# A DMA hold on GpSimd: gradient loads tied to the landing of an x transpose, and a fourth y/z buffer

## Chip, cores, metric

One core of one Trainium2 chip. The metric is the device time of one launch in microseconds, the median of repeated runs. The kernel before takes 2145.0 us (2144.54 to 2149.26 in three runs). All times compared below are of fast runs (not over 1.5% above the fastest of the same kernel) unless it is said otherwise.

## The reference

Window attention over a 256 x 256 image with 384 channels, windows of 8 x 8 tokens, one head; forward output and the gradients of x, wqkv and wo, all bf16.

```python
qkv = xw @ wqkv                       # xw: x cut into windows of 64 tokens
p = softmax(einsum('bqc,bkc->bqk', q, k) * C ** -0.5)
o = einsum('bqk,bkc->bqc', p, v) @ wo
_out, _vjp = jax.vjp(_f, x, wqkv, wo)
return (_out, *_vjp(grad_out))
```

## The kernel before

The image is worked through in 128 quads of eight windows (four 128-token tiles of 96 KB). Each quad needs x and grad_out both with tokens on the partitions (`xq`, `dq`) and with channels on the partitions (`xT`, `dT`). DMA transposes issued by SP turn them; `tok` turns the projections y/z back and `UT` turns a product needed for dx. Four quads are in the pipeline at once, at different steps.

```python
def load(st):
    bp, t0 = st["at"]
    st["xq"] = xq = grp.tile([P, QUAD, C], BF16, tag="xq", name="xq", bufs=2 * GQ + 4)
    st["dq"] = dq = qp.tile([P, QUAD, C], BF16, tag="dq", name="dq", bufs=6)
    for t in range(QUAD):
        nc.sync.dma_start(out=xq[:, t, :], in_=dram_tile(x, bp, t0 + t))
        nc.gpsimd.dma_start(out=dq[:, t, :], in_=dram_tile(grad_out, bp, t0 + t))
# ... cut ...
for i in range(-1, n + 2):
    d, c, b, a = get(i - 2), get(i - 1), get(i), get(i + 1)
    if i + 2 > 0 and get(i + 2) is not None:
        to_channels(get(i + 2), "dq", "dT")       # SP: DMA transpose
        to_channels(get(i + 2), "xq", "xT")       # SP: DMA transpose
    if get(i + LEAD) is not None:                 # LEAD = 3
        load(get(i + LEAD))                       # SP: x, GpSimd: grad_out
    if c is not None:
        to_tokens(c)                              # SP: DMA transpose tok
    step(d, c, b, a)                              # PE, ACT, DVE; GpSimd stores; SP: UT
```

GpSimd's queue also issues all stores of out_0 (from `osb`, four buffers) and out_1 (from `dsb`). The program gives GpSimd these instructions in one order, so a load that waits there holds up the stores behind it.

Of the kernel before, what the change touches and what calls it, by code (L numbers as in the profile page):

```python
# [11 lines left out]
BF16 = mybir.dt.bfloat16  # L12
F32 = mybir.dt.float32

P = 128
WIN = 8
WT = WIN * WIN
QUAD = 4
# [4 lines left out]
def kernel(  # L23
# [12 lines left out]
    nc = tc.nc  # L36
    _, H, W, C = x.shape
    CK = C // P
# [5 lines left out]
    LEAD = 3  # L44
# [3 lines left out]
    qp = ctx.enter_context(tc.tile_pool(name="qp", bufs=2))  # L48
# [52 lines left out]
    def dram_tile(ap, bp, t):  # L101
        return ap[0, 2 * WIN * bp:2 * WIN * (bp + 1), WIN * t:WIN * (t + 1), :]

    LO, HI = slice(0, WT), slice(WT, P)

    def load(st):
        bp, t0 = st["at"]
        st["xq"] = xq = grp.tile([P, QUAD, C], BF16, tag="xq", name="xq", bufs=2 * GQ + 4)
        st["dq"] = dq = qp.tile([P, QUAD, C], BF16, tag="dq", name="dq", bufs=6)
        for t in range(QUAD):  # L110
            nc.sync.dma_start(out=xq[:, t, :], in_=dram_tile(x, bp, t0 + t))
            nc.gpsimd.dma_start(out=dq[:, t, :], in_=dram_tile(grad_out, bp, t0 + t))  # L112

    def to_channels(st, src, name):
        st[name] = dst = qp.tile([P, QUAD, CK, P], BF16, tag=name, name=name, bufs=3 if name == "xT" else 2)
        nc.sync.dma_start_transpose(out=dst[:].rearrange("p t m k -> p (t m) k"),
                                    in_=st[src][:].rearrange("p t c -> p (t c)"))
# [3 lines left out]
    def product(out, lhsT, rhs, start, stop):  # L121
        if split[0]:
            for h in (LO, HI):
                nc.tensor.matmul(out[h], lhsT=lhsT[:, h], rhs=rhs, start=start, stop=stop)  # L124
        else:
            nc.tensor.matmul(out, lhsT=lhsT, rhs=rhs, start=start, stop=stop)  # L126

    def project(st, kind, mo):
        if kind == 0 and mo == 0:
            st["yz"] = qp.tile([P, CK, QUAD, 4, WT], BF16, tag="yz", name="yz", bufs=3)  # L130
        yz = st["yz"]
        wgt, src = ((BT_sb, st["dT"]), (A_sb, st["xT"]))[kind]
        pj = ring.tile([P, QUAD, 2, WT], F32, tag="r", name="pj")
        for m in range(CK):
            product(pj[:].rearrange("p t w k -> p (t w k)"), wgt[:, m, mo * P:(mo + 1) * P], src[:, :, m, :],
                    m == 0, m == CK - 1)
        if kind == 0:
            nc.scalar.copy(out=yz[:, mo, :, 0:4:3, :], in_=pj[:])  # L138
        else:
            nc.scalar.copy(out=yz[:, mo, :, 1:3, :], in_=pj[:])  # L140

    def to_tokens(st):
        st["tok"] = tok = qp.tile([P, CK, QUAD, 2, P], BF16, tag="tok", name="tok")
        nc.sync.dma_start_transpose(out=tok[:].rearrange("p m t b k -> p (m t b) k"),
                                    in_=st["yz"][:].rearrange("p m t s k -> p (m t s k)"))
# [132 lines left out]
    def gf_group(sts):  # L278
        n = len(sts) * QUAD
        for f, rn in enumerate(("Uq", "Wq")):  # L280
            for ma in range(CK):
                pw = ring.tile([P, C], F32, tag="r", name="pg")
                for i in range(n):
                    st, t = sts[i // QUAD], i % QUAD
                    product(pw[:], st["xq"][:, t, ma * P:(ma + 1) * P], st[rn][:, t, :], i == 0, i == n - 1)
                nc.vector.tensor_tensor(out=GF_acc[:, f, ma, :], in0=pw[:], in1=GF_acc[:, f, ma, :], op=ALU.add)  # L286
                yield

    def filler(n):
        while n and fill:  # L290
            try:
                next(fill[0])
                n -= 1
            except StopIteration:
                fill.pop(0)

    def step(d, c, b, a):
        def on(st):
            return (lambda f, *r: f(st, *r)) if st is not None else (lambda f, *r: None)
        D_, C_, B, A = on(d), on(c), on(b), on(a)  # L300
        B(scores)
        B(soft, 0)
        B(soft, 1)
        B(values, 0)
        B(values, 1)
        B(values, 2)
        B(soft, 2)
        B(values, 3)
        B(soft, 3, 0)
        A(project, 0, 0)  # L310
        A(project, 0, 1)
        B(soft, 3, 1)
        A(project, 0, 2)
        B(soft, 4)
        A(project, 1, 0)
        B(soft, 5)
        A(project, 1, 1)
        A(project, 1, 2)
        filler(1)
        pw = C_(attend, (2, 3))  # L320
        pt = B(turn)
        if b is not None:
            turn_end(b, pt)
        C_(to_channels, "Uq", "UT")
        C_(attend_end, (2, 3), pw)
        split[0] = True
        D_(dx, (0, 1))
        filler(1)
        split[0] = False
        pw = B(attend, (0, 1))  # L330
        B(attend_end, (0, 1), pw)
        D_(dx, (2, 3))
# [4 lines left out]
    get = lambda i: sts[i] if 0 <= i < n else None  # L337
    with tc.manual_schedule(engines=MANUAL):
        for i in range(min(LEAD - 1, n)):
            load(sts[i])  # L340
        to_channels(sts[0], "dq", "dT")
        to_channels(sts[0], "xq", "xT")
        held = []
# [3 lines that stand above are left out]
                to_channels(get(i + 2), "dq", "dT")  # L347
                to_channels(get(i + 2), "xq", "xT")
            if get(i + LEAD) is not None:
                load(get(i + LEAD))  # L350
            if c is not None:
                to_tokens(c)
            step(d, c, b, a)
            if c is not None:
                held.append(c)
            if held and (len(held) == GQ or i == n):
                fill.append(gf_group(held))
                held = []
            if 0 <= i - 2:
                sts[i - 2] = None  # L360
        filler(1 << 30)
# [62 lines left out]
```

## Time and profile before

| | before |
|---|---|
| time, median | 2145.0 us |
| PE busy | 2021.4 us, 95% |
| DMA queue shares, SP + GpSimd | 85.6% + 27.5% |
| SP's cycle: one quad, dT to dT | 16.41 us |
| of it in issues / waiting before dT / other gaps | 15.58 / 0.23 / 0.60 us |
| PE's shortest spacing of quads (the first three, shorter, left out); mean of all | 14.83; 16.26 us |

SP's cycle is read out of the trace instruction by instruction (quads 11 to 120), not from a ready view. SP's cycle is the sum of how long its eight issues of a quad last and of the gaps between them. I read a long issue as one whose descriptors the DMA engines don't take at once (tok's lasts 4.08 to 6.78 us for the same work); a gap is a wait for something not yet there. The prediction shows the lines of the profile.

### The profile page before, as it was taken

To read this page: it belongs to the slowest core of one execution; us is meant where nothing else is said; L and a number is where in the kernel's file an instruction comes from. 1 tells how busy PE (TensorE), PEld (TensorE's weight loads), DVE (VectorE), ACT (ScalarE), POOL (GpSimd) and SP (SyncE) were. 2 spreads that over 40 slices of the span, in tenths; PEclk is the share of its full clock that TensorE was granted. 3 is DMA by queue.
4 is the path that set the end of the run, shared out by engine and by line. 5 is a ranking of instruction groups with operands and counts; after the bars stand their busy time and mean duration, and the time that the engine had idled before them with its cause. 6 is when DMAs were issued, how large, how long until landed. Compare 5 with 4: busy or idle time off the path is not lost. (4 is left out here: it accounts for less than half of the span.)

```text
span 2135.8 us, 51378 instructions
## 1 busy us (share of the span) xinstructions
PE 2021.4 (95%) x19046; PEld 1183.3 (55%) x19046; DVE 1280.2 (60%) x2851; ACT 1455.3 (68%) x3213; POOL 1122.7 (53%) x2054
## 2 busy tenths in 40 slices
PE   8899999999999999999999999999999999999998
PEld 4555555555555555555555555555555555555555
DVE  6565565656565656656565665665656565665664
ACT  6667676766676667767676766766666676666673
POOL 4554555555555545545454555554555455555543
PEclk9999999999999999999999999999999999999999
DMA  9999999999999999999999999999999999999995
GB/s 210 220 225 220 217 219 211 224 221 219 215 219 213 225 206 225 218 212 222 215 218 213 216 224 211 218 220 218 216 212 221 211 220 222 222 223 211 220 208 123
DMA packets 1173339, 459.11 MB, mean 215 GB/s; under 512 B 1056864, under 2 KB 1147744, under 8 KB 1173088
## 3 DMA queue, kind: packets, MB, share of 16 engines
q1 hardware_dynamic: 1074384, 304.15, 85.6%
q0 software_dynamic: 98304, 151.39, 27.5%
q8 instruction: 149, 2.44, 0.5%
q14 instruction: 102, 0.84, 0.1%
q10 hardware_dynamic: 400, 0.29, 0.0%
HBM read 101.84 MB, written 101.84 MB: 95 GB/s over the span
## 5 line engine op out<-in xcount | busy, mean ns | idle before, releaser
L231 POOL DMA_DIRECT2D out_dram<-osb x1024 | 578.3, 571 | 682.9 <-ACT osb L249 637.3
L138 ACT CAST yz<-pj 128x512 bf16<-128x512 f32 x384 | 213.4, 588 | 360.6 <-DMA tok<-yz 328.0
L286 DVE TENSOR_TENSOR GF_acc<-pg,GF_acc 128x384 f32<-128x384 f32 x258 | 143.9, 558 | 471.8 <-PE pg L124 269.0
L249 ACT CAST osb<-po 128x384 bf16<-128x384 f32 x512 | 225.1, 501 | 211.3 <-issue 174.8
L112 POOL DMA_DIRECT2D dq<-in_grad_out_dram x512 | 270.6, 537 | 174.2 <-DMA out_dram<-osb 63.8
L233 POOL DMA_DIRECT2D out_dram<-dsb x512 | 275.4, 541 | 136.4 <-DMA out_dram<-dsb 62.4
L250 DVE CAST Uq<-pu 128x384 bf16<-128x384 f32 x512 | 264.7, 550 | 54.9 <-PE pu L242 53.0
L126 PE MATMUL pv<-B_sb,xT 128*128 128x384 bf16 x1536 | 270.6, 326 | 0.0
L126 PE MATMUL pj<-xT,A_sb 128*128 128x512 bf16 x1152 | 269.5, 379 | 0.9 <-DMA xT<-xq 0.9
L126 PE MATMUL pj<-dT,BT_sb 128*128 128x512 bf16 x1152 | 269.5, 379 | 0.0
L224 ACT CAST uq<-pv 128x384 bf16<-128x384 f32 x512 | 242.7, 475 | 35.5 <-PE pv L126 33.3
L261 ACT CAST Wq<-pw 64x384 bf16<-64x384 f32 x512 | 242.5, 474 | 9.2
L273 ACT CAST dsb<-pd 128x384 bf16<-128x384 f32 x512 | 222.0, 482 | 26.0 <-ACT Wq L261 7.5
L124 PEld LDWEIGHTS <-xq 128*64 128x64 bf16 x3024 | 204.6, 111 | 45.6
L126 PEld LDWEIGHTS <-xq 128*128 128x128 bf16 x1560 | 152.6, 98 | 114.0
L140 ACT CAST yz<-pj 128x512 bf16<-128x512 f32 x384 | 201.3, 603 | 1.2 <-PE pj L126 1.1
L126 PEld LDWEIGHTS <-A_sb 128*128 128x128 bf16 x1152 | 112.6, 98 | 137.1 <-DMA xT<-xq 1.4
L242 PE MATMUL po<-uq,PS 64*64 64x384 bf16 x1024 | 145.0, 338 | 45.9 <-ACT yz L138 45.5
L126 PEld LDWEIGHTS <-xT 128*128 128x128 bf16 x1536 | 141.5, 98 | 82.8
L124 PE MATMUL pg<-Wq,xq 128*64 128x384 bf16 x2016 | 182.0, 329 | 0.0
L166 DVE TENSOR_REDUCE mx<-sd 64x4 f32<-64x256 f32 x256 | 108.1, 422 | 122.6 <-PE sd L153 118.6
L126 PE MATMUL pg<-Uq,xq 128*128 128x384 bf16 x1032 | 181.6, 326 | 0.0
(66 smaller groups left out, 2674.9 us busy)
## 6 DMA issues: line engine op xcount, KB each, us to landing
xq<-in_x_dram SPq DMA_DIRECT2D x512, 96.0 KB, 3.7
dq<-in_grad_out_dram POOLq DMA_DIRECT2D x512, 96.0 KB, 4.8
out_dram<-osb POOLq DMA_DIRECT2D x1024, 48.0 KB, 5.3
out_dram<-dsb POOLq DMA_DIRECT2D x512, 96.0 KB, 5.5
dT<-dq SPq DMA_TRANSPOSE x128, 6.5
xT<-xq SPq DMA_TRANSPOSE x128, 5.1
tok<-yz SPq DMA_TRANSPOSE x128, 10.2
UT<-Uq SPq DMA_TRANSPOSE x128, 6.4
```

Source lines behind the costliest of these rows:

```text
L112: nc.gpsimd.dma_start(out=dq[:, t, :], in_=dram_tile(grad_out, bp, t0 + t))
L124: nc.tensor.matmul(out[h], lhsT=lhsT[:, h], rhs=rhs, start=start, stop=stop)
L126: nc.tensor.matmul(out, lhsT=lhsT, rhs=rhs, start=start, stop=stop)
L138: nc.scalar.copy(out=yz[:, mo, :, 0:4:3, :], in_=pj[:])
L140: nc.scalar.copy(out=yz[:, mo, :, 1:3, :], in_=pj[:])
L224: nc.scalar.copy(out=st["uq"][:, t, :], in_=pj[:])
L231: nc.gpsimd.dma_start(out=to[WIN * w:WIN * (w + 1)], in_=src[h, :])
L233: nc.gpsimd.dma_start(out=to, in_=src[:])
L249: nc.scalar.copy(out=osb[:], in_=po[:])
L250: nc.vector.tensor_copy(out=st["Uq"][:, t, :], in_=pu[:])
L261: nc.scalar.copy(out=st["Wq"][h, pair[1], :], in_=pw[1][o, :])
L273: nc.scalar.copy(out=dsb[:], in_=pd[:])
```

## The change

The intent: keep the gradient loads away from the transposes dT and xT and let them run beside the plain x loads that follow these. A one-element copy on GpSimd reads `xT` of the quad two on and writes into the gradient tile, so it can't run before that transpose has landed, and the loads behind it can't start before the copy.

```diff
-    def load(st):
+    def load(st, behind=None):
...
+        if behind is not None:
+            nc.gpsimd.tensor_copy(out=dq[0:1, 0, 0:1], in_=behind["xT"][0:1, 0, 0, 0:1])
         for t in range(QUAD):
...
-            st["yz"] = qp.tile([P, CK, QUAD, 4, WT], BF16, tag="yz", name="yz", bufs=3)
+            st["yz"] = qp.tile([P, CK, QUAD, 4, WT], BF16, tag="yz", name="yz", bufs=4)
...
-                load(get(i + LEAD))
+                load(get(i + LEAD), get(i + 2))
```

## The prediction

> **What bounds the kernel now.** I read the page first, then the waits, then the timeline of the SP queue, because the first two do not name one bound.
>
> ```profile
> PE 2021.4 (95%) x19046; PEld 1183.3 (55%) x19046; DVE 1280.2 (60%) x2851; ACT 1455.3 (68%) x3213; POOL 1122.7 (53%) x2054
> ...
> DMA  9999999999999999999999999999999999999995
> ...
> q1 hardware_dynamic: 1074384, 304.15, 85.6%
> q0 software_dynamic: 98304, 151.39, 27.5%
> ```
>
> PE and the DMA engines both look full. PE is not the bound: with no stall, one quad takes PE 14.83 us from its scores to the next quad's (the smallest spacing of the sd matmuls, seen in 20-odd of 127 quads), while the mean spacing is 16.26 us. What is lost shows in the waits, where ACT holds PE up because a y/z buffer still belongs to a transpose:
>
> ```profile
> ACT yz L138 <- DMA tok<-yz: 328.0, 99, 7.2
> PE po L242 <- ACT yz L138: 45.5, 72, 3.9
> ```
>
> The columns are total us, times and longest us. Why are the transposes late? This is the SP queue, one quad from dT to dT being the repeating unit (start, duration):
>
> ```profile
> 1009.94 3.12 SPq L116 DMA_TRANSPOSE dT<-dq  x1
> 1013.24 1.69 SPq L116 DMA_TRANSPOSE xT<-xq  x1
> 1014.98 2.89 SPq L111 DMA_DIRECT2D xq<-in_x_dram  x4
> 1017.98 6.78 SPq L144 DMA_TRANSPOSE tok<-yz  x1
> 1024.85 2.88 SPq L116 DMA_TRANSPOSE UT<-Uq  x1
> 1027.95 1.80 SPq L116 DMA_TRANSPOSE dT<-dq  x1
> ```
>
> It is never idle: each issue begins within 0.3 us of the end of the one before, and between 80 us and 2,078 us I find no gap over 0.4 us. It waits for no semaphore; it is busy issuing. The mean issue times are 5.44 (tok), 2.46 (UT), 2.88 (dT), 2.18 (xT) and four x loads of 0.66: 15.6 us, which with some 0.7 us between them is the whole 16.3 us quad. So the SP stream sets the pace and PE follows it. Most of that time is not forced. The same issues by tile (min/median/max ns):
>
> ```profile
> L144 SPq DMA_TRANSPOSE tok<-yz x128: 4077/5442/6779, 36.1 to 2099.2; - x128
> L116 SPq DMA_TRANSPOSE UT<-Uq x128: 1422/2477/3950, 41.3 to 2103.7; - x128
> L116 SPq DMA_TRANSPOSE dT<-dq x128: 1447/2918/3953, 9.3 to 2060.4; - x128
> L116 SPq DMA_TRANSPOSE xT<-xq x128: 1413/2229/3890, 11.1 to 2063.5; - x128
> ```
>
> At the minima a quad would take 4.1 + 1.4 + 1.4 + 1.4 + 4 x 0.55 + 0.7 = 11.2 us. The other 5 us are back-pressure, as GpSimd's queue (q0: gradient loads and both outputs' stores, 12 x 96 KB a quad) uses the same DMA engines. Stretches show how badly the two mix (last columns: DMA share, GB/s):
>
> ```profile
> 1004.50:1006.50 2.00, 2.00 (x25) 1.03 (x22) 1.93 (x4) 1.65 (x4) 1.15 (x3) 1.00 1.14 56
> 1026.00:1027.00 1.00, 1.00 (x6) 0.41 (x5) 0.95 (x3) 0.00 (x0) 0.26 (x1) 1.00 1.09 365
> 1031.00:1033.00 2.00, 1.07 (x9) 0.46 (x10) 0.81 (x2) 2.00 (x5) 0.00 (x0) 1.00 1.27 286
> ```
>
> By the packet records, the third is transposes alone, the second q0 alone with the transposes standing, and the first is tok's transposes beside a few store packets: everything in flight, next to nothing moved.
>
> **What the Trainium skill says.** "DMA: Bandwidth & Descriptors", section "Issuing engines are not separate DMA queues": transfers begun from any engine end up on the same 16 DMA engines and interleave. The trace agrees: the two queues' shares sum to 113%. The same page, "Queues, rings and completion order": an engine takes turns between queues, a packet at a time. A transpose packet (256 B) takes 18 ns in the median and 174 ns at the 99th percentile; a q0 packet of 4,608 B takes 178 ns at its fastest. A transpose packet that waits out one q0 packet would look like that. "Perfetto Trace Analysis", "Identifying Performance Opportunities": a bubble that repeats can mean too few buffers. The 99 waits of ACT for tok are such a bubble, but the next part says why I expect little from the buffer.
>
> **The change part by part.** *Fourth y/z buffer.* The write of y/z then waits for a transpose issued one quad earlier, long landed; the 328 us of ACT's wait, and PE's 45.5 + 13.4 us of waits for ACT's yz casts, go. But the SP stream does not wait for PE: its inputs (yz, dq, xq) are ready many us before it gets to them. PE therefore runs ahead by a few us once, until it stands at dx for UT (landing now 8.2 us after the start of the step that needs it about 10 us in), and then again moves at SP's pace. Alone: nothing, 0 to 10 us.
>
> *The hold.* It adds 126 one-element GpSimd copies (GpSimd's memsets in this trace took 0.1 to 0.2 us; estimate 0.2 to 0.3 us each with their semaphores, on an engine that is idle at that moment). It takes no transfer away; it moves them. Times below are from L, the landing of xT (13.0 us into PE's step in the mean). Now the four gradient loads are issued from L - 8.8 us; their data flow, some 3 us later (median from issue to first large packet 2.94 us), during the UT, dT and xT transposes. Afterwards they are issued from L + 0.4 to L + 2.5. The x loads are issued from about L - 3 to L - 0.4 and their packets run from about L - 0.9 to L + 1.8. GpSimd has been idle, so the first data come about 1 us after issue: the tail of the x loads catches perhaps 60 KB, and the rest runs beside tok, which follows at once. The intent of running beside x is met only in part. GpSimd is in order, so the stores of osb, which now run beside the x loads, fall in behind: osb at L + 2.5 to 4.8, dsb to 5.9, osb to 8.2, dsb to 9.3.
>
> To price this I cut the SP queue's data stream into phases by its own packets and fitted each phase's length, over 115 quads, to the KB of each kind of q0 traffic in it. Mean KB a quad (gradients, osb, dsb), length without q0, and us per 1,000 KB:
> x loads: 12, 134, 30; 1.95 us; 4.25, 4.79, 2.08.
> tok: 1, 115, 143; 4.62; (no gradients to fit), 1.96, 3.06.
> UT: 77, 125, 153; 2.26; 4.17, 3.25, 2.71.
> dT: 132, 7, 53; 1.27; 6.77, 9.74, 4.82.
> xT: 162, 5, 6; 1.69; 4.91, 2.60, 5.62.
> Measured lengths 2.70, 5.29, 3.40, 2.49, 2.53: 16.41 us. The reason for the differences I take to be that tok and x are issued slower than the engines could move them and leave room, and dT and xT do not.
>
> After, with my placing (x 60 gradients; tok 324 gradients and 192 osb; UT 192 dsb and 150 osb; dT 42 osb and 192 dsb; xT none), and 3.34 us per 1,000 KB for gradients in tok, which is tok's slope for all traffic together:
> x 1.95 + 0.26 = 2.21; tok 4.62 + 1.08 + 0.38 = 6.08; UT 2.26 + 0.52 + 0.49 = 3.27; dT 1.27 + 0.41 + 0.93 = 2.61; xT 1.69. Sum **15.86 us**, 0.55 less than 16.41. Over some 127 quads: **70 us**, 2145 - 70 = **2075 us**.
>
> A second reading of the same trace: sorted by q0 traffic within dT and xT, the quarter of the quads with least (142 KB) took 15.68 us a cycle, the others 16.46, 16.69 and 16.81 (316, 436, 568 KB), at nearly equal totals. After the change I place 234 KB there. That agrees in sign and size: about 0.5 us.
>
> **Rivals.** *Only moved.* If gradients cost as much beside tok as beside dT and xT (5.7 us per 1,000 KB instead of 3.34), tok grows by another 0.76 us and the sum is 16.6: no gain, 2145 to 2175. For it: tok's fit is weak (R2 0.16), a fit over whole cycles gives tok traffic 5.5 +- 2 us per 1,000 KB, and the empty stretch shown above lies in tok. Against it: the quarters.
> *A new loop.* xT's landing, copy, gradient loads, dT, xT is now a ring: 0.4 to the first issue, 1.6 to the fourth, about 4.5 to its landing (the median is 4.8), 2.9 and 2.2 for the two issues, 3 to the landing: 14.6 us, near the cycle. SP would reach dT at L + 7.8 and the gradients land at about L + 6.5. A wait of SP there of up to 2 us is filled by UT's packets still queued (2.6 us from issue to first packet), so I expect short waits and little loss. If landings stretch to 7 us beside tok, it adds up to 1 us a quad: slower, up to 2200.
> *Stores late.* osb has four buffers; stores now leave some 4 to 6 us later and would land about L + 9, against the next use at about L + 12. ACT's osb may begin to wait for DMA, but PE has slack against SP, so this costs nothing unless several us more are lost.
> *Better than placed.* If dT and xT free of q0 come down to their minima and tok swallows the gradients in its own slack, the cycle falls towards 15 us, and PE at 14.83 us becomes the bound: 1970 to 2000.
>
> **Range and chances.** The main sum says 2075, the first rival 2145 or a little over, the last 2000. The fits are correlations in one trace, so I widen both ways and move the middle a little towards no change: 2080 us, 8 in 10 for 2005 to 2150. Faster by over 2% means below 2102: 0.60. Within 2%: 0.34. Slower: 0.06.
>
> **What would show it.** Right: ACT's wait for tok on yz gone, SP still without gaps, dT and xT issues down from 2.9 and 2.2 us to about 2.3 and 1.5, tok up towards 6, spacing of the sd matmuls about 15.8 us, the PE's stalls now at dx for UT or tok. Wrong: gaps on SP before dT that a gradient load ends (the loop), tok far above 6.5 us (only moved), PE at 14.83 us throughout (SP was not autonomous, or the buffer mattered), or ACT's osb waiting for stores with PE behind it. The step I trust least is the price of gradients beside tok.

## The result, and the profile after

The changed kernel takes 2239.76 us (2225.55 to 2252.35, three runs): ratio 1.0433, 95% interval 1.0331 to 1.0535, **slower**. Ratios here are the mean time of one kernel's fast runs over the mean of the other's of the same rounds, so not quite the ratio of the quoted medians. The prediction was 2080 us in a range of 2005 to 2150.

The page of the changed kernel, busy times and DMA queues:

```profile
PE 2021.8 (90%) x19046; PEld 1127.7 (50%) x19046; DVE 1264.2 (56%) x2851; ACT 1466.8 (66%) x3213; POOL 1145.3 (51%) x2180
...
q1 hardware_dynamic: 1074384, 304.15, 80.5%
q0 software_dynamic: 98304, 151.39, 28.1%
```

The work is the same to the packet, and PE is as busy in microseconds as before; there is more time in which it waits. (The granted clock reads 0.971 after and 0.986 before; with PE's busy time the same within 0.4 us, the lost time is not there.) What SP waits for, before (total us, times, longest):

```profile
SPq L116 <- DMA dq<-in_grad_out_dram: 1.3, 2, 0.9
```

and after:

```profile
SPq L118 <- DMA dq<-in_grad_out_dram: 225.4, 235, 4.6
```

This wait was not there before. It stands in front of dT, the transpose of the gradients. The view has longer lines for SP in both kernels (before: `SPq L144 <- ACT uq L224`, 349.0 us), but most of that lies within issues: the gaps before tok sum to 19 us in the whole run before. The gaps before dT sum to 30 us before and 251 after, which bears out the line above. SP's queue after, one cycle in order of time (start, duration):

```profile
1018.98 4.38 SPq L146 DMA_TRANSPOSE tok<-yz  x1
1023.45 1.99 SPq L118 DMA_TRANSPOSE UT<-Uq  x1
1027.17 1.44 SPq L118 DMA_TRANSPOSE dT<-dq  x1
1028.79 2.87 SPq L118 DMA_TRANSPOSE xT<-xq  x1
1031.71 4.77 SPq L113 DMA_DIRECT2D xq<-in_x_dram  x4
```

UT's issue ends at 1025.44 and dT's begins at 1027.17: SP stands still for 1.7 us. Every other gap in these lines is 0.2 us or less. GpSimd in the same stretch:

```profile
1019.41 0.18 POOL L111 COPY dq<-xT 1x1 bf16<-1x1 bf16 x1 [5.10 <-PE pw L244]
1019.97 2.11 POOL L114 DMA_DIRECT2D dq<-in_grad_out_dram  x4 [0.39 <-POOL dq L111]
1022.05 2.28 POOL L233 DMA_DIRECT2D out_dram<-osb  x4
1026.42 1.08 POOL L235 DMA_DIRECT2D out_dram<-dsb  x2 [2.09 <-DMA dq<-in_grad_out_dram]
```

The copy comes 5.1 us after GpSimd's last work, the loads are issued from 1019.97 on, but their data don't flow then. Counted from the packet records of the same stretch (half-microsecond slices; transpose packets started, KB of GpSimd's queue started):

```
from     transposes  x loads  GpSimd's queue
1020.5   362         8        0 KB
1022.0   568         0        0 KB
1023.0   521         0        0 KB
1024.0   237         0        63 KB
1025.0   8           0        156 KB
1026.0   0           0        117 KB
1027.0   502         0        0 KB     gradients landed, dT issued
```

Four loads, all issued by 1022.1, move nothing until tok's transposes run out, from about 1024 on; then they and the first stores behind them have the engines to themselves while the transposes stand. The two kinds of traffic take turns in blocks.

The durations of the issues after (ns, min/median/max), and the gradient loads with their median time from issue to landing (last number, us; it was 4.8 before):

```profile
L146 SPq DMA_TRANSPOSE tok<-yz x128: 3808/4290/7587, 42.6 to 2201.5; - x128
L118 SPq DMA_TRANSPOSE dT<-dq x128: 1423/1594/2957, 9.2 to 2166.0; - x128
L118 SPq DMA_TRANSPOSE xT<-xq x128: 1431/2932/4277, 10.9 to 2167.6; - x128
...
dq<-in_grad_out_dram POOLq DMA_DIRECT2D x512, 96.0 KB, 6.0
```

Against the lines in the prediction, tok is 1.15 us and dT 1.3 us shorter, and xT is 0.7 us longer. The mean over quads (a quad's four x loads included) gives the balance: issues 14.65 us instead of 15.58, waiting before dT 1.95 instead of 0.23, other gaps 0.59: a cycle of **17.19 us instead of 16.41**. The difference of 0.78 us over 127 quads is 99 us; the measured slowdown is 95.

Two more lines of the changed kernel's waits, which a rival explanation rests on:

```profile
ACT osb L251 <- DMA out_dram<-osb: 381.0, 210, 5.9
...
PE pd L269 <- DMA tok<-yz: 78.6, 57, 6.5
```

ACT now waits for an osb buffer whose store is late, and PE waits for tok at dx.

### The profile page after: what moved, and what is told of

It reads as the page before. It is cut to its first block, busy times and chain, and to the rows that moved or that the text cites.

```text
span 2238.0 us, 51758 instructions
## 1 busy us (share of the span) xinstructions
PE 2021.8 (90%) x19046; PEld 1127.7 (50%) x19046; DVE 1264.2 (56%) x2851; ACT 1466.8 (66%) x3213; POOL 1145.3 (51%) x2180
## 5 line engine op out<-in xcount | busy, mean ns | idle before, releaser
L251 ACT CAST osb<-po 128x384 bf16<-128x384 f32 x512 | 236.5, 480 | 645.9 <-DMA out_dram<-osb 381.0
L111 POOL COPY dq<-xT 1x1 bf16<-1x1 bf16 x126 | 22.4, 178 | 608.9 <-DMA xT<-xq 400.8
L269 PE MATMUL pd<-tok,ps 128*64 128x384 bf16 x1024 | 144.8, 339 | 137.9 <-DMA tok<-yz 78.6
L252 DVE CAST Uq<-pu 128x384 bf16<-128x384 f32 x512 | 259.3, 548 | 14.7 <-PE pu L244 14.5
L275 ACT CAST dsb<-pd 128x384 bf16<-128x384 f32 x512 | 227.4, 481 | 57.5 <-PE pd L126 19.6
L226 ACT CAST uq<-pv 128x384 bf16<-128x384 f32 x512 | 233.5, 483 | 18.4 <-PE pv L128 16.6
L126 PEld LDWEIGHTS <-xq 128*64 128x64 bf16 x3024 | 191.7, 120 | 91.8
L126 PE MATMUL pd<-AT_sb,UT 128*64 128x384 bf16 x1536 | 174.0, 369 | 57.3 <-DMA UT<-Uq 56.4
L140 ACT CAST yz<-pj 128x512 bf16<-128x512 f32 x384 | 220.5, 589 | 3.9 <-PE pj L128 0.2
L142 ACT CAST yz<-pj 128x512 bf16<-128x512 f32 x384 | 201.3, 603 | 0.2
L126 PE MATMUL pg<-Wq,xq 128*64 128x384 bf16 x2016 | 195.2, 347 | 0.0
```

What stands on the lines that cost most here:

```text
L126: nc.tensor.matmul(out[h], lhsT=lhsT[:, h], rhs=rhs, start=start, stop=stop)
L140: nc.scalar.copy(out=yz[:, mo, :, 0:4:3, :], in_=pj[:])
L142: nc.scalar.copy(out=yz[:, mo, :, 1:3, :], in_=pj[:])
L226: nc.scalar.copy(out=st["uq"][:, t, :], in_=pj[:])
L251: nc.scalar.copy(out=osb[:], in_=po[:])
L252: nc.vector.tensor_copy(out=st["Uq"][:, t, :], in_=pu[:])
```

## The experiments

**Theories.** *Ring*: the hold closes a ring, from xT's landing through the copy, the gradient loads and SP's wait at dT to the issue and landing of the next xT. Measured from xT's landing, means of quads 10 to 119: first load issued at 0.72, the fourth at 2.38, the last landed at 8.65, dT issued at 8.79 us. With 1.81 for dT's issue, 0.19 for the gap and 6.4 from xT's issue to its landing (the page's median) that is 17.2 us, the whole cycle. *Contention*: bunching GpSimd's transfers makes the DMA engines slower whatever waits there are. *Late stores*: the stores behind the hold come late, osb's four buffers run out, ACT and PE fall behind. *Buffer*: the fourth y/z buffer lets PE run ahead into something worse.

A summary of all runs first; cycle, issues and waits are SP's, in us a quad, each from the profiled run of that kernel:

| run | median us | ratio to before | cycle | issues | wait at dT |
|---|---|---|---|---|---|
| before | 2145.0 | 1 | 16.41 | 15.58 | 0.23 |
| the change | 2239.76 | 1.0433 | 17.19 | 14.65 | 1.95 |
| yz_only | 2149.44 | 0.9984 | 16.47 | 15.65 | 0.23 |
| hold_only | 2274.49 | 1.0590 | 17.38 | 14.70 | 2.08 |
| hold_dT | 2179.32 | 1.0124 | 16.65 | 15.62 | 0.44 |
| hold_lead4 | 2130.02 | 0.9905 | 16.38 | 15.66 | 0.24 |
| free_lead4 | 2145.74 | 0.9972 | 16.43 | 15.71 | 0.23 |
| hold_past | 2132.89 | 0.9910 | 16.36 | 15.53 | 0.24 |
| swap_hold | 2180.47 | 1.0105 | 16.73 | 15.84 | 0.23 |
| swap_free | 2160.03 | 1.0020 | 16.56 | 15.68 | 0.22 |
| tok_split | 2269.74 | 1.0565 | 17.41 | 16.33 | 0.35 |
| split_free | 2225.32 | 1.0346 | 17.16 | 16.20 | 0.23 |
| dose_hold | 2314.56 | 1.0754 | 17.82 | 13.70 | 3.53 |
| dose_lead4 | 2088.13 | 0.9729 | 16.01 | 15.28 | 0.24 |
| lead4_9 (the same again) | 2094.42 | 0.9699 | 16.03 | 15.30 | 0.24 |
| lead4_18 | 2099.81 | 0.9729 | 16.06 | 15.30 | 0.24 |
| lead4_27 | 2392.66 | 1.1084 | 18.56 | 14.54 | 0.33 |

Also run: no_dsb, x_on_act and swap_hold_lead4, told below. In the runs made together, before itself has medians of 2149.6 to 2158.1 us.

### yz_only and hold_only: the two halves

yz_only is the kernel before with `bufs=4` for yz; hold_only is the change with `bufs=3`.

> The fourth y/z buffer alone, no hold. Loop theory (the hold makes SP wait for gradients that themselves wait behind tok): the buffer is innocent; SP sets the pace and does not wait for PE, so the time stays at 2145 us, within 2135 to 2155, and ACT's 328 us of waits for tok on yz go and turn into PE waits for tok or UT at dx. If the buffer is what slows the changed kernel (PE running ahead, stores falling into other transposes): 2200 us or more.

> The hold alone, three y/z buffers. Loop theory: as slow as the whole change or a little slower, 2225 to 2270 us, with SP waiting about 2 us a quad for the gradients before dT. If the buffer is the culprit: 2145 us.

yz_only: 2149.44 us, ratio 0.9984 (0.9959 to 1.0008): as before, within the expectation. hold_only: 2274.49 us, ratio 1.059 (1.0516 to 1.0664), just above the expected range. The buffer theory falls, and the hold alone carries the slowdown. With the hold the fourth buffer even helps, by 35 us; without it, the ring of the profiled run is longer by 0.2 us (the last gradients land at 8.85 us, dT is issued at 9.01), but why was not tested.

The packet records of yz_only show more than its time. PE runs ahead, GpSimd with it, and the gradient loads are issued 12.6 us before xT's landing instead of 8.9. So the buffer alone takes two thirds of the gradients away from dT and xT (100 KB a quad there instead of 294; the table under lead4_9 has both runs), and the time stays. Taking them away from dT and xT was what the hold was for.

### hold_lead4 and free_lead4: the ring opened, everything else kept

```diff
-    LEAD = 3
+    LEAD = 4
-  xq ... bufs=2 * GQ + 4
+  xq ... bufs=2 * GQ + 5
```

hold_lead4 is the change with this edit: the gradients are issued at the same place, after xT and before tok, but belong to the quad after the next. free_lead4 has the edit and the fourth y/z buffer without the hold.

> The whole change with x and gradients loaded one quad further ahead (LEAD 4, one more xq buffer): same hold, same place of the gradient loads between xT and tok, but the dT that needs them comes one quad later, so the ring of hold, gradients, dT, xT is opened. Loop theory: no waits of SP before dT; a quad costs SP its issues, 14.6 us now, and 0.7 us between them, so about 15.4 us a quad: 2010 to 2080 us. Contention or late-store theory: 2200 us or more, as nothing about the mixing or the stores is changed.

> Control for hold_lead4: loads one quad further ahead and four y/z buffers, without the hold. If the hold's new place for the gradients is worth something by itself, this run stays at the time before, 2140 to 2155 us, and hold_lead4's 1 per cent is the hold's. If the 1 per cent came from the longer lead, this run is at 2125 to 2135 us as well.

hold_lead4: 2130.02 us, ratio 0.9905 (0.9879 to 0.9932). SP's wait in this run, and the wait that the late-store theory goes by:

```profile
SPq L118 <- DMA dq<-in_grad_out_dram: 2.4, 2, 1.3
...
ACT osb L251 <- DMA out_dram<-osb: 260.8, 174, 4.8
```

The loads are issued 0.73 us after xT's landing and land at 8.60, as in the change (0.72 and 8.65); only nobody waits for them. The whole slowdown is gone. ACT still waits 261 us for stores, so that wait alone does not slow the kernel. This decides between ring and contention, and between ring and late stores. But the expected 2010 to 2080 us did not come: SP's issues went from 14.65 back to 15.66 us. The short issues of the changed kernel were no gain of the new place. While SP stands, the DMA engines work off what is queued and take the next descriptors faster; that is my reading of 14.65 against 15.66, and of dose_hold below. free_lead4, at 0.9972 (0.9953 to 0.999), shows that the longer lead is not what matters. Against it hold_lead4 is 0.7% faster, about 15 us, where the prediction had 70; and hold_past below, whose loads don't wait, gains as much over yz_only, so even this is not shown to come from the place.

### hold_dT: the hold on the other transpose

```diff
-  in_=behind["xT"][0:1, 0, 0, 0:1]
+  in_=behind["dT"][0:1, 0, 0, 0:1]
```

> The whole change, but the hold waits for the transpose dT of two quads on, which lands some 3 us before xT. Loop theory: the gradient loads are issued while xT is under way, pass at the border of xT and the x loads instead of behind tok, land some 5 us earlier against SP's dT, and SP's waits before dT all but vanish: 2060 to 2140 us. Contention theory (any hold packs GpSimd's traffic into fewer microseconds and the DMA engines lose more): 2200 us or more, SP without waits but with longer issues. Late-store theory (osb's four buffers): 2200 or more, with ACT's osb waiting for stores as now (381 us).

2179.32 us, ratio 1.0124 (1.0067 to 1.0182). SP's wait and the gradient loads' time to landing:

```profile
SPq L118 <- DMA dq<-in_grad_out_dram: 38.1, 46, 2.5
...
dq<-in_grad_out_dram POOLq DMA_DIRECT2D x512, 96.0 KB, 3.5
```

SP's waits fall from 225 us to 38, and most of the slowdown with them; the loads land 2.5 us sooner, no longer behind tok. Here the intent is met: by the packet records 312 of a quad's 384 KB of gradients flow in the x phase. (A phase runs from the last packet of SP's DMA before to the last packet of its own; what flows while the transposes stand counts to the phase that follows.) And it gains nothing: the kernel is still 1.2% slower than before. Against yz_only, its control, the x phase grew from 3.16 to 3.49 us and tok's from 5.19 to 5.46, UT's shrank from 3.55 to 2.95, and the issues sum to 15.62 us as ever; the wait of 0.21 us a quad that is left makes 27 us. The expected time of 2060 to 2140 us was missed.

### hold_past: the copies without the wait

```diff
-                load(get(i + LEAD), get(i + 2))
+                load(get(i + LEAD), get(i + 1))
```

> The whole change, but the copy reads the xT of one quad on instead of two quads on, which landed a quad earlier: the same 126 copies and the same instruction order on GpSimd, with no time in the wait. Loop theory: 2140 to 2160 us, as with the fourth buffer alone; SP waits for gradients below 10 us in all. If the copies themselves, or the order they force, cost the time: 2200 us or more.

2132.89 us, ratio 0.991 (0.9883 to 0.9936), a little better than expected. The copies and their order cost nothing. That they gain 0.7% over yz_only is not explained.

### swap_hold, swap_free, swap_hold_lead4: xT before dT

```diff
-                to_channels(get(i + 2), "dq", "dT")
                 to_channels(get(i + 2), "xq", "xT")
+                to_channels(get(i + 2), "dq", "dT")
```

> The whole change, with SP issuing the transpose xT before dT instead of after it. Hold, buffers, lead and bytes are as in the change, but the gradients now have from the landing of xT to the dT of the next quad about 12.8 us (16.3 us a quad + 2.9 for xT's issue - 6.4 from its issue to its landing) where they had about 7.8 and need about 8.3 (0.7 copy, 1.6 issues, 6.0 landing). Loop theory: SP's waits for gradients fall from 225 us to below 20, and the time to 2120 to 2165 us. Contention or late-store theory: 2200 us or more.

> Control for swap_hold: four y/z buffers and xT before dT, no hold. The order of two equal transposes moves no work: 2135 to 2160 us. If the order itself is worth something, this run shows it and swap_hold must be read against this one.

> hold_lead4 with xT before dT: with no ring left in either, this tells whether the hold's place for the gradients (now released while dT is under way, so nearer to the x loads) is worth more than the 1 per cent of hold_lead4. If DMA work is conserved wherever the gradients run: 2120 to 2150 us. If running truly beside the x loads is the gain that was intended: 2100 us or less.

swap_hold: 2180.47 us, ratio 1.0105 (1.0078 to 1.0131); SP's wait for gradients is 1.0 us in the whole run. As the ring arithmetic said, the last gradients land at 8.0 us and dT is issued at 13.6 us after xT's landing. So the ring opens and most of the slowdown goes, with the lead and the bytes of the change; the time is 15 us above the range, since the issues are 0.16 us longer than in swap_free (2160.03 us, 1.002). swap_hold_lead4: 2175.66 us, ratio 1.0076 (1.0054 to 1.0098), slower than both of its expectations. With no ring in either, running in the x phase (299 of 384 KB in swap_hold) is again no gain.

### dose_hold and dose_lead4: the ring made longer, closed and open

```diff
-            nc.gpsimd.tensor_copy(out=dq[0:1, 0, 0:1], in_=behind["xT"][0:1, 0, 0, 0:1])
+            for _ in range(9):
+                nc.gpsimd.tensor_copy(out=dq[0:1, 0, 0:1], in_=behind["xT"][0:1, 0, 0, 0:1])
```

> The whole change with the one-element copy done nine times in a row instead of once: every gradient load is issued later by eight more copies, 1.4 us if they follow each other at their 178 ns, more if each waits for the one before. Loop theory: the ring sets the cycle (17.2 us), so nearly all of the delay shows in each of some 126 quads: 2240 + 126 x 1.4 = about 2410 us, 2340 to 2450. Contention or late-store theory: a delay of an idle GpSimd engine changes little, 2220 to 2290 us.

> The same nine copies in hold_lead4, where the gradients have a whole quad to spare. Loop theory: nothing to delay, 2120 to 2160 us. If the delay costs as much here as in dose_hold, the ring is not what it acts through.

dose_hold: 2314.56 us, ratio 1.0754 (1.0718 to 1.079), 75 us more than the change, below the expected range. The loads are issued 1.89 us later but land only 0.71 us later, since the last one takes 5.10 us to land instead of 6.27; 0.71 us over 126 quads is 89 us. SP's wait in this run:

```profile
SPq L119 <- DMA dq<-in_grad_out_dram: 419.2, 249, 6.2
```

dose_lead4: 2088.13 us, ratio 0.9729 (0.9658 to 0.98). The same delay costs 75 us where the ring is closed and gains 42 where it is open. That settles the ring, and it contradicts what I had expected of the open one, no effect. It is also faster than both kernels.

### lead4_9, lead4_18, lead4_27: how late is best

hold_lead4 with 9 (a repeat of dose_lead4), 18 and 27 copies.

> A repeat of dose_lead4, same source, beside two longer delays. If its gain is real: 2075 to 2105 us again; if it was chance: 2130 us, as hold_lead4.

> Eighteen copies in hold_lead4: the gradients are issued some 4.6 us after xT's landing instead of 2.7 (nine copies) or 0.7 (one). In dose_lead4 the tok transpose, nearly free of other traffic, took 3.8 us of data instead of 4.7 and the gradients passed behind it. If keeping tok to itself is the gain, the best is near where they arrive at tok's end, so about as dose_lead4, 2070 to 2110 us. If any delay gains (less traffic bunched with the stores): lower still, below 2070.

> Twenty-seven copies: gradients issued some 6.6 us after xT's landing, into UT and dT, with the osb stores a further 2 us late behind them on GpSimd. If tok to itself is the gain: no better than with 18, 2090 to 2150 us, as UT, dT and xT now carry what tok was spared and ACT's osb waits longer for its buffers. If any delay gains: below 2070.

lead4_9: 2094.42 us, ratio **0.9699** (0.9675 to 0.9724); the gain is real. lead4_18: 2099.81 us, 0.9729 (0.9696 to 0.9762), the same. Where the gradients flow, in KB a quad and in SP's data phases (which are cut at SP's own packets), with each phase's length in us (two counts of one run differ by up to some 20 KB in tok and UT):

```
             x     tok          UT           dT           xT
before       2.71  5.30 (1)     3.41 (68)    2.48 (132)   2.48 (162)
yz_only      3.16  5.19 (5)     3.55 (267)   2.15 (83)    2.42 (17)
free_lead4   3.07  5.32 (5)     3.53 (284)   2.13 (75)    2.39 (8)
hold_lead4   2.49  4.70 (160)   3.82 (215)   2.33 (2)     3.03 (0)
lead4_9      2.83  3.72 (59)    3.99 (299)   2.57 (18)    2.94 (1)
lead4_18     2.91  4.31 (12)    2.82 (108)   3.32 (201)   2.72 (52)
```

With nine copies they reach the engines as tok ends. tok, left nearly alone, is 0.98 us shorter, and the others give back 0.66. So a place can matter, but it is not the one beside the x loads. Two quite different places, UT and dT, give the same time, so this is a reading for nine copies and no rule.

lead4_27: 2392.66 us, ratio 1.1084, far outside the 2090 to 2150 expected. GpSimd in this run:

```profile
1015.72 6.39 POOL L112 COPY dq<-xT 1x1 bf16<-1x1 bf16 x27
1022.47 2.11 POOL L115 DMA_DIRECT2D dq<-in_grad_out_dram  x4 [0.37 <-POOL dq L112]
1024.55 2.28 POOL L234 DMA_DIRECT2D out_dram<-osb  x4
1029.63 1.08 POOL L236 DMA_DIRECT2D out_dram<-dsb  x2 [2.80 <-DMA dq<-in_grad_out_dram]
1030.70 2.25 POOL L234 DMA_DIRECT2D out_dram<-osb  x4
1032.95 1.08 POOL L236 DMA_DIRECT2D out_dram<-dsb  x2
1034.02 6.15 POOL L112 COPY dq<-xT 1x1 bf16<-1x1 bf16 x26
```

It no longer waits for xT at all: 15.2 us of its own work and 2.8 of a wait fill the cycle. Stores come later still, PE waits 266.9 us behind ACT's osb, and SP stands 3.2 us a quad before UT. Here the late-store theory holds, once GpSimd itself is full.

### tok_split and split_free: tok in three pieces

```diff
-  one DMA transpose of all of yz into tok
+  for m in range(CK): one DMA transpose of yz[:, m] into tok[:, m]
```

> The whole change, with the tok transpose cut into three, one for each third of the channels. The packet records show GpSimd's packets passing mostly near the borders between two transposes, and the held gradients land late (median 5.8 us) because tok, the longest, stands in front of them. If that is what stretches the ring: gradients land about 1 us sooner, SP's wait for them before dT falls from 225 us to below 120, and the time to 2150 to 2200 us. If their lateness has another cause (start-up of GpSimd's queue, bandwidth alone): waits and time as in the change, 2225 to 2260 us.

> Control for tok_split: fourth y/z buffer, tok cut in three, no hold. If the cut itself is what kept tok_split slow (its SP issues sum to 16.4 us a quad where uncut kernels without waits have 15.6): 2230 to 2280 us, as slow as tok_split. If the cut is free: 2145 us, and then tok_split's time is unexplained by the ring.

tok_split (the change with this edit): 2269.74 us, ratio 1.0565 (1.0524 to 1.0606). The gradients land at a median of 4.6 us instead of 6.0 (the 5.8 of the expectation has dT's own landings mixed in) and SP's wait for them falls to 23.1 us from 225.4, as expected if tok stands in their way; the packet records agree, as the first load of a quad starts to move data 1.53 us after its issue (median), in the change 3.59 us and in hold_dT, beside the x loads, 1.32 us. The time does not fall. split_free (the edit without the hold): 2225.32 us, 1.0346, 5 us below its range. Three smaller transposes make SP's issues dearer by 0.55 us a quad (16.20 against 15.65 in yz_only), which hides what the ring gave back: the hold costs 44 us with tok cut (2269.74 against 2225.32) and 90 us uncut (2239.76 against 2149.44). So the pair supports the reason for the late landing, and half of the cost goes with it; SP's waits account for some 15 us of the 44 that are left, the rest is not explained.

### no_dsb and x_on_act: what sets SP's pace

no_dsb is the kernel before without most stores of out_1. Its output is wrong, which doesn't matter for the time. x_on_act is yz_only with the x loads issued by ACT (`nc.scalar.dma_start`).

> Wrong result on purpose: the kernel before with the stores of out_1 left out from the second band of windows on, a third of GpSimd's traffic. If the DMA engines' total work sets the pace (16.3 us a quad, of which some 1.4 to 1.7 us for 384 KB), PE becomes the bound at 14.83 us a quad or nearly: 1950 to 2010 us. If PE or a chain of waits sets the pace: 2100 us or more.

> Fourth y/z buffer, no hold, and the x loads issued from ScalarE's queue instead of SP's: takes four issues of 0.7 us a quad out of the SP stream without changing a byte. If the SP queue's own issuing is the pace, a quad falls to PE's 14.83 us: 1960 to 2030 us. If the DMA engines' work is the pace, the transposes' issues stretch by what was freed and the time stays within 2 per cent of 2145 us.

no_dsb: 2092.81 us in one run of unknown state, cycle 16.05 us. With a third of GpSimd's traffic gone, the cycle is 0.36 us shorter where 1.4 to 1.7 were expected. Neither expectation holds: as far as one run goes, traffic costs, but not by the KB. x_on_act: 2229.7 us, ratio 1.0317 (1.0237 to 1.0397), also outside both expectations. SP has four issues fewer, and its transposes' issues stretch from 12.74 us a quad (yz_only) to 16.49. So SP's issuing time is not what the pace is made of; but the load on ACT, whose casts PE waits for, changed as well, so the slowdown itself is not explained by this run.

## Why the prediction was wrong

**What sets the pace: right as far as tested.** SP's stream led before and leads after: what was lost stands in its gaps before dT. Its cycle accounts for the slowdown, 0.78 us x 127 = 99 us against 95 measured; that sum alone does not show who leads, since in the long run all engines have the same cycle. (The prediction's "no gap over 0.4 us" is a slip: I count ten gaps of 0.42 to 0.56 us between 80 and 2,078 us, too few to matter.)

**Fourth buffer: right in time.** "Alone: nothing, 0 to 10 us"; measured 0.9984. Missed was that GpSimd runs ahead with PE, so that the buffer moves the gradients by itself.

**The hold, where the gradients flow: both the places and the prices were wrong.** The sum of 15.86 us failed first in its placing. I placed 324 KB of gradients beside tok and nothing in xT; in the change 192 KB flowed beside tok and 176 beside UT. hold_lead4 has the place without the ring, and its phases sum to 16.37 us. tok is shorter than summed (4.70 against 6.08), xT carries some 300 KB of stores and takes 3.03 us instead of 1.69, and UT carries 215 KB of gradients and takes 3.82 instead of 3.27. The prediction's prices at the KB that did flow give 16.38 us for hold_lead4, which is right; but they give 15.94 for yz_only, where 16.47 was measured, and 16.94 for lead4_9, where it was 16.0. A price list that misses by 0.5 to 0.9 us could not carry a gain of 0.55. In the changed kernel's own trace the same fit gives 10.4 us per 1,000 KB for gradients in tok instead of 3.34; I take it that phases that end when GpSimd's block gets its turn have their length and their KB from a common cause. Sorting the quads by KB was no second witness: the quarters come out as printed if a cycle is cut before the x loads, but cut before UT they are 16.48, 16.13, 16.23 and 16.73 us, and the quarter with least traffic gains nothing.

**The ring: named, priced, and dismissed.** The prediction has it as a rival with "about 4.5 to its landing" and "up to 1 us a quad: slower, up to 2200". This is the step that made the change slower. The landing was the mis-sized term: the last load took 6.27 us, since tok stood before it, so the gradients landed at 8.65 us after xT's landing and not at 6.5. The "about 1 us" from issue to first data was 3.59 us for the first load (median). xT took 6.4 us from issue to landing instead of the 5.2 summed; dT's issue, 1.81 instead of 2.9, nearly makes up for that. SP would have reached dT at 7.8. "A wait of SP there of up to 2 us is filled by UT's packets still queued" was wrong by half: the wait grew by 1.72 us, the issues shrank by 0.93, and 0.78 stayed. That term of the prediction should have been computed with the landing behind tok, which the prediction itself had put there. And a chance of 0.06 for slower was too small for a ring that I had summed to 14.6 us with a mean landing in it.

**Late stores: right that they cost nothing here.** ACT's wait appeared (381 us), and hold_lead4 has 261 us of it at 0.9905; PE's own wait behind it at dx is 50.0 us in the change and 43.9 in hold_lead4.

**What stays open.** Why the copies alone gain 0.7% (hold_past) and with that whether hold_lead4's 0.7% is the place's, why the fourth buffer helps by 35 us beside the hold, and why UT and dT are equally good places for the gradients in lead4_9 and lead4_18.

## What to carry to other kernels

Before a transfer is held behind an event, follow what the held data release and see whether the path comes back to that event; if it does, add up the ring with the landing time that the transfer will have at its new place, not the one it has now. If it closes near the cycle, load one round further ahead before trying the hold: the same hold went from 4.3% slower to no loss (0.9905), and with nine copies of delay to 3% faster. And a fit of times against traffic within one trace is weak evidence for moving the traffic; a run that moves it and opens the ring is cheap.

## What the Trainium skill lacked or had wrong

- "DMA: Bandwidth & Descriptors", "Queues, rings and completion order", describes turns between queues a packet at a time. Beside long DMA transposes this case shows turns in blocks: in the changed kernel four loads issued by 1022.1 us start no data until about 1024, at tok's end, and of the large packets of GpSimd's queue that start during tok's data phase 69% (2,494 of 3,598) start in its last fifth. The section says nothing of transposes; whether the trace's packets are the page's is not known here.
- The same page, "Anatomy of one DMA — SWDGE (gpsimd) path", fits a single DMA as 2.0 us and its bytes over 436 GB/s, an estimate of 2.2 us for 96 KB. The trace agrees for the quickest gradient load (2.2 us); the median was 6.0 and the longest 11.2 us, and it was that lateness that mattered.
- I found no page that says what it costs to cut a DMA transpose in pieces. Cutting one of 24 blocks of 128 x 128 in three cost 0.55 us of SP's issues a quad and 3.5% of the time.
- A row of one-element copies on GpSimd is a usable delay: eight more copies put the loads off by 1.89 us, 236 ns each (178 ns of it busy), and the DMA behind the last starts 0.39 us after it in the change. I found no page with the delay that such a row makes.
